# A last column range of one whole block, a final store from the scalar queue, and a new order of the early work in a fused attention and MoE kernel

## Chip, cores and metric

One core of a Trainium2 chip. The metric is the device time of a run in microseconds (us), lower is better. A profiled run's "span" is about 1.8 us shorter than its time, because it starts at the program's first instruction and ends at its last.

## The reference

Sliding-window attention with a linear distance bias, followed by a two-layer MLP with a squared ReLU:

```python
# q, k, v: (8, 8, 576, 64) float32
scores = (1/8) * q @ k.T + slope[h] * -(pos_q - pos_k)
scores = where(0 <= pos_q - pos_k < 128, scores, -1e9)
x = softmax(scores) @ v                     # (8, 8, 576, 64)
x = x.transpose(0, 2, 1, 3).reshape(4608, 512)
h = x @ w_in                                # (512, 2048)
out = (relu(h) ** 2) @ w_out                # (2048, 512), float32
```

Each batch has 576 positions: four blocks of 128 and a half block of 64. With a window of 128, a block attends to itself and to the block before it.

## The kernel before

A small list scheduler in the kernel plans the whole program: every piece of work is a task with engines, a key (priority), dependencies and ring slots. It then emits the instructions in the order of the planned starts. Each engine works through its own list strictly in that order.

The 40 blocks are numbered by when they are loaded: 0 to 7 are the first blocks of the eight batches, 8 to 13 are full blocks, 14 and 15 half blocks, and so on. For each block, keys and queries are loaded into one of four `kq` buffers, transposed (`kqT`), multiplied (scores `s`), exponentiated and masked (`P`), multiplied by `v` (`pv`), normalised (`x`), and transposed into columns of `xT`. The MLP then takes 512 columns at a time: `h` (with `w_in`, four loaded parts), relu and square (`g`), and `o` (with `w_out`, four parts).

```python
N_PE = 9            # blocks 0 to 8 are transposed on TensorE, the others by DMA
SIZE = {"kq": 4, "v": 9, "kqT": 7, "P": 3, "x": 3}
...
def load_block(m, key):                       # block m
    s_kq[m], s_v[m] = Slot("kq"), Slot("v" if kb else "v0")
    ...
    def fetch_kq():
        for i, src in enumerate((k, q)):
            nc.gpsimd.dma_start(view(kq[s_kq[m].idx], i), source(src, m, split))
...
def transpose_kq(m, due):
    if m >= N_PE:                             # by DMA, from the sync queue
        def flip():
            nc.sync.dma_start_transpose(out=tile_of(sT)[:, :, 0:n], in_=kq[s_kq[m].idx][0:n, :])
        t_f = plan.add({"SP": 1500.0}, due - 60, flip, ..., [sT], [s_kq[m]], ...)   # frees kq[m] when it lands
        return
    ...                                       # else 8 matmuls with the identity, which free kq[m]
...
if m >= N_PE:                                 # x of block m into xT, also from the sync queue
    def flip_x():
        nc.sync.dma_start_transpose(out=xT[:, :, t0:t0 + n], in_=xt[sx.idx][0:n, :])
...
# columns: the two half blocks of a pair of batches share one range of 128 columns,
# so the last range of all is two half blocks
        jobs.append(("half", [len(seq), len(seq) + 1]))
        ranges.append([(b, HALF), (b + 1, HALF)])
        seq += ranges[-1]
...
# the last 128 rows of the output are cut at column 384; each piece is stored per block of its range
def store():
    for i, (b, kb) in enumerate(ranges[4 * g + t]):
        nc.sync.dma_start(out[b * S + kb * 128:b * S + kb * 128 + n, lo:hi], so.tile[i * 64:i * 64 + n, 0:hi - lo])
```

`fill` puts matmuls without use into planned gaps of TensorE in the first 30 us.

The softmax here doesn't subtract the row's maximum and nothing guards it: scores larger than these inputs give would overflow.

## Time and profile before

| | |
|---|---|
| time, first 3 runs | 317.85 us median (317.34 to 317.96) |
| span of the profiled run | 315.63 us |
| TensorE busy | 306.2 us, 97% |
| last matmul ends | 311.02 us |
| last matmul to the end | 4.61 us |

From the page of the kernel before, its busy line, and two rows of its 40 slices (one digit is the busy share of a slice of 7.9 us, in tenths):

```profile
PE 306.2 (97%) x2810; PEld 176.3 (56%) x2810; DVE 173.4 (55%) x494; ACT 173.5 (55%) x340; POOL 105.4 (33%) x131
...
PE   6989999999999999999999999999999999999994
...
DMA  9999999999999999999999949962211000011112
```

Only slices 1, 3 and 40 of the TensorE row are under 9: after about 33 us the engine has no wait until its last matmul. DMA is at 90% or more in 25 of the first 26 slices, to about 205 us. It is no bound as long as TensorE finds its data.

The waits of TensorE alone, kernel before (total us, times, longest):

```profile
PE tp L443 <- DVE kq L379: 1.9, 1, 1.9
PE wm L413 <- DVE warm L291: 1.2, 1, 1.2
PE h L700 <- ACT rt L671: 0.7, 1, 0.7
PE h L700 <- DMA w_in_sb<-in_moe_w_in_dram: 0.3, 1, 0.3
PE o L742 <- DMA w_out_sb<-in_moe_w_out_dram: 0.3, 1, 0.3
PE pv L566 <- ACT kqf L273: 0.3, 1, 0.3
```

These are all of TensorE's waits, 4.7 us in total, none after 33 us.

The end, from the timeline of the kernel before (start, duration, engine, operation, idle before it):

```profile
310.17 0.56 DVE L271 COPY osb<-o 128x384 f32<-128x384 f32 x1 [1.85 <-PE o L742]
310.75 2.41 SPq L761 DMA_DIRECT2D out_dram<-osb  x4
311.06 0.29 DVE L271 COPY osb<-o 128x128 f32<-128x128 f32 x1 [0.34 <-PE o L742]
```

The last copy is done at 311.35, but the sync queue (SPq) is busy with four store issues until 313.16. In the trace they start at 310.75, 311.29, 311.98 and 312.57 and take 0.49, 0.59, 0.54 and 0.59 us. The last lands at 314.49.

### The profile page before, as it was taken

The page shows a single profiled execution, that of the slowest core. Times are in us where ns is not written, and L with a number is a line of the kernel's source. Part 1 is how long each engine was busy: PE and PEld are TensorE (multiplying, and loading weights), DVE is VectorE, ACT ScalarE, POOL GpSimd, SP SyncE. Part 2 cuts the span into 40 slices and gives each one's busy share as a digit, 9 for nine tenths or more (in the row PEclk, how much of TensorE's full clock was granted, in tenths as well). Part 3 has the DMA queues.
Part 4 walks back from the last instruction along what each step waited for, and adds up shares of the span by engine and source line. Part 5 has one row for each costly group of instructions (what it writes and reads, how often), then busy time and mean ns, then how long its engine had stood idle before and what let it go on. Part 6 is the DMA issues. An engine that isn't in the chain of part 4 may idle for free.

```text
span 315.6 us, 7140 instructions
## 1 busy us (share of the span) xinstructions
PE 306.2 (97%) x2810; PEld 176.3 (56%) x2810; DVE 173.4 (55%) x494; ACT 173.5 (55%) x340; POOL 105.4 (33%) x131
## 2 busy tenths in 40 slices
PE   6989999999999999999999999999999999999994
PEld 2878767667777655555555455545444444444442
DVE  3755567666767667676676666666663222222111
ACT  4676466668566635675655665557743444444300
POOL 8825498643623837206756007200000000000000
PEclk9799999999999999999999999999999999999999
DMA  9999999999999999999999949962211000011112
GB/s 129 190 204 190 169 194 178 141 174 127 208 178 127 172 136 194 160 118 143 160 199 160 145 96 137 190 114 70 50 52 50 35 34 33 35 33 44 57 69 66
DMA packets 164130, 39.14 MB, mean 124 GB/s; under 512 B 154752, under 2 KB 159616, under 8 KB 164096
## 3 DMA queue, kind: packets, MB, share of 16 engines
q0 software_dynamic: 114656, 18.10, 84.3%
q1 hardware_dynamic: 49152, 20.33, 34.3%
q8 instruction: 22, 0.36, 0.5%
q10 hardware_dynamic: 288, 0.26, 0.3%
q14 instruction: 12, 0.10, 0.1%
HBM read 36.70 MB, written 9.44 MB: 146 GB/s over the span
## 4 chain that ended last, share of the span: by engine, by line
PE 86%; DMA 9%; POOL 2%; issue 0%; DVE 0%; POOLq 0%
PE o L742 38%; PE h L716 27%; PE h L700 10%; PE pv L566 6%; PE s L499 5%; DMA w_out_sb<-in_moe_w_out_dram 5%; DMA w_in_sb<-in_moe_w_in_dram 3%; DMA kq<-in_q_dram 2%; POOL kq L387 1%; POOL vf L392 1%; PE tp L443 0%; PE xp L608 0%; POOL w_in_sb L340 0%; POOL dist L287 0%; DVE osb L271 0%
## 5 line engine op out<-in xcount | busy, mean ns | idle before, releaser
L742 PE MATMUL o<-w_out_sb,g 128*128 128x512 bf16 (+2 forms) x592 | 143.0, 373 | 0.3 <-DMA w_out_sb<-in_moe_w_out_dram 0.3
L671 ACT ACTIVATE rt<-h 128x512 bf16<-128x512 f32 x144 | 85.8, 609 | 94.2 <-PE h L716 69.9
L662 DVE TENSOR_TENSOR g<-rt 128x512 bf16<-128x512 bf16 x144 | 60.2, 421 | 75.7 <-ACT rt L671 75.6
L716 PE MATMUL h<-xT,w_in_sb 128*128 128x512 bf16 x384 | 96.7, 379 | 0.0
L742 PEld LDWEIGHTS <-g 128*128 128x128 bf16 x592 | 54.0, 98 | 55.9 <-issue 0.4
L523 ACT ACTIVATE P<-s 128x512 bf16<-128x512 f32 (+1 forms) x136 | 67.0, 582 | 9.0 <-PE s L499 8.9
L716 PEld LDWEIGHTS <-w_in_sb 128*128 128x128 bf16 x384 | 35.2, 98 | 39.3
L531 DVE TENSOR_TENSOR P<-P,masks 128x512 bf16<-128x512 bf16 (+1 forms) x112 | 44.6, 405 | 15.1 <-ACT P L523 10.3
L700 PE MATMUL h<-xT,w_in_sb 128*128 128x128 bf16 (+1 forms) x512 | 46.8, 246 | 1.1 <-ACT rt L671 0.7
L387 POOL DMA_DIRECT2D kq<-in_k_dram x39 | 33.5, 858 | 33.5 <-DMA kqT<-kq 28.2
L392 POOL DMA_DIRECT2D vt<-in_v_dram x32 | 27.0, 847 | 45.8 <-PE pv L566 43.5
L700 PEld LDWEIGHTS <-w_in_sb 128*128 128x128 bf16 x512 | 38.6, 98 | 5.2 <-DMA w_in_sb<-in_moe_w_in_dram 1.4
L387 POOL DMA_DIRECT2D kq<-in_q_dram x39 | 33.5, 859 | 9.1 <-PE h L700 4.8
L588 DVE TENSOR_TENSOR x<-pv,rec 128x256 bf16<-128x256 f32 (+1 forms) x80 | 33.5, 422 | 2.6
L566 PEld LDWEIGHTS <-P 128*128 128x128 bf16 (+1 forms) x576 | 26.0, 101 | 15.2 <-DVE x L588 1.7
L584 DVE RECIPROCAL rec<-pv 128x4 f32<-128x4 f32 (+1 forms) x80 | 14.2, 179 | 21.0 <-PE pv L566 18.1
L566 PE MATMUL pv<-vt,P 128*128 128x65 bf16 (+1 forms) x448 | 24.6, 194 | 0.0
L273 ACT ACTIVATE osb<-o 128x512 f32<-128x512 f32 x23 | 13.9, 606 | 8.0 <-PE o L742 7.7
L499 PEld LDWEIGHTS <-kqT 64*128 64x128 bf16 x448 | 12.4, 94 | 7.3 <-issue 7.2
L271 DVE COPY osb<-o 128x512 f32<-128x512 f32 (+2 forms) x14 | 9.2, 654 | 12.8 <-PE o L742 12.6
L499 PE MATMUL s<-kqT 64*128 64x128 bf16 (+1 forms) x256 | 15.6, 210 | 0.0
L499 PE MATMUL s<-kqT,kqT 64*128 64x128 bf16 (+1 forms) x192 | 11.4, 209 | 0.0
(42 smaller groups left out, 103.1 us busy)
## 6 DMA issues: line engine op xcount, KB each, us to landing
out_dram<-osb SPq DMA_DIRECT2D x32, 256.0 KB, 4.0
kq<-in_k_dram POOLq DMA_DIRECT2D x31, 128.0 KB, 7.2
kq<-in_q_dram POOLq DMA_DIRECT2D x31, 128.0 KB, 7.4
vt<-in_v_dram POOLq DMA_DIRECT2D x24, 128.0 KB, 7.4
w_in_sb<-in_moe_w_in_dram POOLq DMA_DIRECT2D x4, 512.0 KB, 11.0
w_out_sb<-in_moe_w_out_dram POOLq DMA_DIRECT2D x4, 512.0 KB, 14.4
vf<-in_v_dram POOLq DMA_DIRECT2D x8, 128.0 KB, 6.7
out_dram<-osb SPq DMA_DIRECT2D x6, 128.0 KB, 2.3
```

Of the source, the lines that this page charges most:

```text
L387: nc.gpsimd.dma_start(view(kq[s_kq[m].idx], i), source(src, m, split))
L392: nc.gpsimd.dma_start(tile_of(s_v[m])[0:n, :, 0:D], source(v, m))
L499: nc.tensor.matmul(sS[2 * g2 + r].tile[:, jj * 256 + c0:jj * 256 + c0 + w], tile_of(s_kqT[mk])[rows, c, :], tile_of(s_kqT[mq])[rows, C + c ...
L523: nc.scalar.activation(flat(Pt[sP.idx]), sS[i].tile.rearrange("p (j t) -> p j t", j=2)[:, :, lo:hi], AF.Exp, bias=0.0, scale=scale)
L531: nc.vector.tensor_tensor(flat(Pt[sP.idx]), flat(Pt[sP.idx]), flat(masks), op=ALU.mult)
L566: nc.tensor.matmul(sv.tile[0:n, hi * (D + 1):(hi + 1) * (D + 1)], Pt[sP.idx][:, place(h)].rearrange("p t q -> p (t q)")[:, w], tile_of(s_v ...
L588: nc.vector.tensor_tensor(xt[sx.idx][0:n, hf * 256:(hf + 1) * 256].rearrange("p (h e) -> p h e", h=4), heads(sv)[0:n, :, 0:D], sr.tile[0:n ...
L662: nc.vector.tensor_tensor(o, i, i, op=ALU.mult)
L671: nc.scalar.activation(srt.tile, slot.tile, AF.Relu, bias=0.0, scale=1.0)
L700: nc.tensor.matmul(slot.tile[:, f * w:(f + 1) * w], w_in_sb[:, cc, fc * 128:(fc + 1) * 128], xT[:, cc, lo:lo + w], start=cc == 0, stop=cc ...
L716: nc.tensor.matmul(slot.tile, w_in_sb[:, cc, fc * 128:(fc + 1) * 128], xT[:, cc, g * 512:(g + 1) * 512], start=cc == 0, stop=cc == C - 1)
L742: nc.tensor.matmul(slot.tile[:, 0:hi - lo], gt[:, fc, t * 128:(t + 1) * 128], w_out_sb[:, fc, lo:hi], start=fc == 0, stop=fc == FCB - 1)
```

## The change

Three intents: (1) the last column range becomes a whole block, so that each of the last two pieces is one store, and the very last is copied on ScalarE and issued from its queue; (2) the order of the early units is searched anew, by adding offsets to single tasks' keys; (3) one block fewer is transposed on TensorE (`N_PE` 9 to 8). `LEAD`, `DUE`, `NEAR` and `N_CUT` belong to the second: when the attention work of a block is due, within how many ns of the earliest start a task with a better key is preferred, and for how many blocks x is transposed in two halves.

```diff
-FIRST = ["b0", "b1", "b2", "i0", "i1", "o0", "i2", "o1", "b3", "i3", "o2", "o3", "b4", "b5", "b6", "b7"]
+FIRST = ["b0", "b1", "b2", "i0", "i1", "o0", "i2", "b3", "i3", "o1", "o2", "o3", "b4", "b5", "b6", "b7"]
-N_PE = 9
-N_CUT = 4
+N_PE = 8
+N_CUT = 2
-LEAD = 320
+LEAD = 1160
-DUE = {**{m: 200.0 * m - 1e5 for m in range(40)}, **{7: -40.0}}
+DUE = {m: 200.0 * m - 1e5 for m in range(40)}
+ADJ = {
+    "e1.1": 9000135.6, "e19.2": -177.01, ..., "u0.1.1": -99420.7, "u0.2.1": -99696.3, ...
+}
-    NEAR = {"PE": 25, "ACT": 250, "DVE": 60}
+    NEAR = {"PE": 60, "ACT": 0, "DVE": 25}
     def order(self):
+        for t in self.tasks:
+            t.key += ADJ.get(t.name, 0.0)
-        ranges.append([(b, HALF), (b + 1, HALF)])
-        seq += ranges[-1]
+        seq += [(b, HALF), (b + 1, HALF)]
+
+        ranges.insert(len(ranges) - (b + 2 == B), seq[-2:])
+        engs = {"ACT": act(hi - lo), "DVE": dve_p(hi - lo)}
+        if end and (g, t) == (NG - 1, 3):
+            del engs["DVE"]
+        final = end and (g, t) == (NG - 1, 3)
-                nc.sync.dma_start(out[...], so.tile[...])
+                (nc.scalar if final else nc.sync).dma_start(out[...], so.tile[...])
# cut: new names of tasks, a stage ring of one buffer, planning dependencies, release of g by all four last pieces
```

## The prediction

> **What bounds it now.** The page gives TensorE 306.2 of 315.6 us busy, and the table by stretches shows it 100% busy from 50 us to the last matmul at 311.06. Before that, the waits view and timeline show 1.2 us of start, a 1.9 us wait for the q cast (5.2 to 7.06), later waits of 0.3, 0.7, 0.3 and 0.3 us, and 54 filler matmuls (about 3 us). At the end, 4.6 us pass between the last matmul and the end. So only useful TensorE work, TensorE time lost before 33 us and the tail can change the time.
>
> **What the change does (from the built order of instructions).**
> 1. One block fewer (the ninth) is transposed on TensorE: 8 key/query and 4 x transposes go to the DMA queue. Four take 0.22 us in the timeline, so 0.66 us is removed. Fillers go from 54 to 50.
> 2. Weight w_out part 1 is loaded after block 3 and w_in part 3. Loads land back to back (0.85 us per block tensor, about 2.5 us per weight part), so w_in part 3 should land near 27.4 us instead of 29.96, block 3's q near 24.0 instead of 26.5.
> 3. Block 2's scores and all of block 1's attention come before the first h matmul. That first h is tied to w_in part 0 (landed 14.23; h began 14.34), the third h unit to part 1 (landed 17.76; began 17.80). These do not move. After them I expect waits of about 0.9 us (part 1) and 0.6 us (part 3), much as before; but the work done by about 37 us is one h unit (0.9 us) more and 0.4 us sooner: 1.3 us ahead.
> 4. Block 8's keys now come by DMA transpose. Block 9's took 8.4 us (51.80 to 60.20). Block 8's q lands about 49, so its transpose lands 56.9 to 57.7; TensorE would reach those scores at about 56.8. I expect a new wait of 0 to 0.9 us here, giving back part of step 3.
> 5. Tail: the last range is one store per piece instead of two. Now the scalar copy ends about 311.35, but the last of four sync-queue issues starts at 312.57 (0.5 to 0.6 us each), lands 314.49, end 315.63. One issue on the scalar queue at about 311.45, landing 1.9 us later, saves 1.1 us. The Trainium skill ("Trainium Kernel Development and Optimization", Key Constraints) says that several issuing engines only save issue time: what is saved here.
> 6. Attention stands 2.5 to 5 us of h and o work later relative to the rest, so the middle should keep having no waits; the larger lead changes little.
>
> The trace also has one half-clock stretch of 3.41 us (8.42 to 11.84), the window length in the Trainium skill ("TensorE: Matmul & The Clock Gate", Part 1). The new filler may prevent it; worth at most a few tenths, as the first h waits for weights.
>
> **Sum.** Last matmul 309.2 to 310.1 (gain 1.0 to 1.9), tail 1.1: gain 2.1 to 3.0 us. Predicted 315.2 us, 8 in 10 between 313.6 and 316.9. Faster by over 2%: 0.02; within 2%: 0.97; slower: 0.01.
>
> **Right if:** last matmul near 309.6; last landing 2.2 to 2.4 us after it (before: 3.4); w_in part 3 lands near 27.4; a TensorE wait at block 8's first scores under 1 us; none from 60 us on.
>
> **Wrong if:** that transpose lands late (1 to 3 us lost, near no gain); the new ACT and DVE order stalls TensorE for h or o banks; or early waits vanish altogether (2 us more gain).

## More of the kernel before

The sync queue (SPq) between 60 and 80 us, kernel before. The transposes of keys (`kqT`) and of x (`xT`) share it with the stores:

```profile
...
64.35 1.31 SPq L429 DMA_TRANSPOSE kqT<-kq  x1
67.88 1.25 SPq L596 DMA_TRANSPOSE xT<-x  x1
73.25 2.56 SPq L429 DMA_TRANSPOSE kqT<-kq  x2
...
```

The first line shown is block 12's keys, the second block 9's x. That x was ready at 67.85 (end of its normalisation on VectorE) and was issued at once.

## The result, and the profile after

| | before | after |
|---|---|---|
| time, median of 4 runs | 317.60 us (317.32 to 317.96) | 316.52 us (316.23 to 317.28) |
| ratio | | 0.9969 (0.9947 to 0.9991) |
| span of the profiled run | 315.63 | 314.45 |
| last matmul ends | 311.02 | 311.44 |
| last matmul to the end | 4.61 | 3.00 |

A ratio is the mean time of one kernel's fast runs over the mean of the other's fast runs of the same rounds, so it is not quite the ratio of the medians.

The change gains 1.1 us; I had predicted about 2.6. The last two rows say more: TensorE ends 0.4 us *later* than before, and the shorter end makes up for it. The early part, from which I expected 1.0 to 1.9 us, gave nothing.

The busy line of the page after:

```profile
PE 306.3 (97%) x2794; PEld 176.0 (56%) x2794; DVE 174.1 (55%) x498; ACT 170.7 (54%) x331; POOL 105.5 (34%) x131
```

The waits of TensorE alone, kernel after:

```profile
PE h L721 <- DMA w_in_sb<-in_moe_w_in_dram: 2.3, 2, 1.4
PE wm L434 <- DVE warm L308: 1.2, 1, 1.2
PE h L721 <- DMA xT<-x: 0.7, 1, 0.7
PE tp L464 <- DMA kq<-in_q_dram: 0.4, 1, 0.4
PE pv L587 <- ACT P L544: 0.4, 1, 0.4
PE xp L629 <- DVE x L609: 0.2, 1, 0.2
```

The early waits are different ones, of about the same size. The third line is new in kind: `h` waits for a DMA transpose of x. Where, the timeline of TensorE after tells:

```profile
14.99 1.07 PE L721 MATMUL h<-xT,w_in_sb 128*128 128x128 bf16 x16 [0.93 <-DMA w_in_sb<-in_moe_w_in_dram]
...
17.56 1.89 PE L721 MATMUL h<-xT,w_in_sb 128*128 128x128 bf16 x16 [1.40 <-DMA w_in_sb<-in_moe_w_in_dram]
...
80.52 2.79 PE L721 MATMUL h<-xT,w_in_sb 128*128 128x256 bf16 x24 [0.65 <-DMA xT<-x]
```

In the first two lines, the first `h` unit waits for weight part 0 (landed 14.94) and the second already for part 1 (landed 17.52). The third line is at 80.52, where I had expected no wait at all. There is no later one.

The sync queue between 60 and 80 us, kernel after:

```profile
61.71 1.23 SPq L450 DMA_TRANSPOSE kqT<-kq  x1
63.72 1.20 SPq L617 DMA_TRANSPOSE xT<-x  x1
73.12 1.23 SPq L450 DMA_TRANSPOSE kqT<-kq  x1
74.45 1.29 SPq L617 DMA_TRANSPOSE xT<-x  x1
...
```

The queue issues nothing from 64.9 to 73.12, then block 12's keys, then block 9's x at 74.45, although that x was ready at 70.06. The waits of the queue itself name what held it, the load of block 12's keys (its queries landed 0.7 us later, at 73.11):

```profile
SPq L450 <- DMA kq<-in_k_dram: 7.5, 1, 7.5
```

The x transpose lands at 80.48, and TensorE goes on at 80.52.

The chain of waits in the stretch from 60 to 100 us (shares by line), before and then after:

```profile
by line: PE h L700 49.9%; PE o L742 31.3%; PE pv L566 9.8%; PE s L499 8.3%; PE xp L608 1.1%
```

```profile
by line: PE h L721 45.7%; PE o L766 26.2%; DMA xT<-x 15.1%; PE s L520 7.0%; PE pv L587 6.2%; issue 0.1%
```

Before, the chain through this stretch is TensorE alone; after, it runs through a transfer from 74.45 to 80.48. Before 74.45 the view goes back to TensorE, but there it can't be trusted: it takes a VectorE event at 75.65, after the transpose had been issued, for what released it. The queue's own wait above is the better guide.

The end, from the timeline after:

```profile
310.59 0.56 DVE L288 COPY osb<-o 128x384 f32<-128x384 f32 x1 [1.85 <-PE o L766]
311.48 0.28 ACT L290 ACTIVATE osb<-o 128x128 f32<-128x128 f32 x1 [13.26 <-PE o L766]
311.79 0.35 ACTq L790 DMA_DIRECT2D out_dram<-osb  x1
```

One issue of 0.35 us, started at 311.79 and landed at 313.35, in place of the end of a row of four.

### Where the wait at 80 us comes from

Reading the loads and the transposes of the two traces side by side (us):

| | before | after |
|---|---|---|
| block 8's keys and queries have landed | 49.2 | 48.9 |
| block 8's buffer is read to the end | 49.8 (TensorE) | 57.40 (DMA transpose, issued 48.98) |
| block 12's k and q loads, same buffer, issued | 52.64, 53.76 | 58.68, 61.98 |
| they land | 61.80, 64.30 | 72.40, 73.11 |
| block 12's key transpose issued | 64.35 | 73.12 |
| block 9's x ready | 67.85 | 70.06 |
| block 9's x transpose issued | 67.88 | 74.45 |
| it lands | 76.36 | 80.48 |
| TensorE waits for it | no | 0.65 |

Theory A: the time is set at 80 us by a transfer. Block 8's DMA transpose holds a key buffer 7.6 us longer than TensorE did. The scheduler, which plans with that, put the v loads of blocks 12 to 16 ahead of block 12's keys and queries, which land 9 us later. (That order comes from `N_PE`, and not from the new offsets: building the kernel before with `N_PE = 8` alone, which was not run, gives the same order of these loads, and all the kernels here with `N_PE = 9` have block 12's load first. On the chip the delay goes through that order: the buffer was free at 57.40, and the waits just before the two loads, issued at 58.68 and 61.98, end with the landings of earlier loads, at 58.38 and 61.69.) Block 12's key transpose waits for it at the head of the sync queue, and block 9's x transpose stands behind. The Trainium skill ("DMA: Bandwidth & Descriptors", Anatomy of one DMA, written for the GpSimd path) says that "any semaphore wait happens on the issuing sequencer before dispatch"; the trace agrees for the sync queue, with 4.4 us (70.06 to 74.45) in which a ready transfer was not issued. What TensorE gains before 80 us is then waited away.

Theory B: the early part itself is the loss. TensorE waits 0.93 and 1.40 us for weights. In the profiled run a half-clock stretch also fell on the `h` units that follow (17.20 to 20.61), where before it fell on the prelude (8.42 to 11.84). The wait at 80 us is then a side effect worth its 0.65 us.

### The profile page after: what moved, and what is told of

Its sections match the earlier page's. It is cut to its first block, busy times and chain, and to the rows that moved or that the text cites. A ratio compares the mean times of both kernels' runs of the same rounds, so it can differ in the third digit from the quotient of the medians.

```text
span 314.4 us, 7113 instructions
## 1 busy us (share of the span) xinstructions
PE 306.3 (97%) x2794; PEld 176.0 (56%) x2794; DVE 174.1 (55%) x498; ACT 170.7 (54%) x331; POOL 105.5 (34%) x131
## 4 chain that ended last, share of the span: by engine, by line
PE 92%; DMA 5%; POOL 2%; issue 0%; ACT 0%; POOLq 0%
PE o L766 39%; PE h L739 27%; PE h L721 14%; PE pv L587 6%; PE s L520 5%; DMA w_in_sb<-in_moe_w_in_dram 3%; DMA xT<-x 2%; POOL kq L408 1%; POOL vf L413 1%; PE tp L464 1%; PE xp L629 0%; POOL w_in_sb L357 0%; POOL dist L304 0%; ACT osb L290 0%; POOLq L304 0%
## 5 line engine op out<-in xcount | busy, mean ns | idle before, releaser
L721 PE MATMUL h<-xT,w_in_sb 128*128 128x128 bf16 (+1 forms) x512 | 47.9, 250 | 3.0 <-DMA w_in_sb<-in_moe_w_in_dram 2.3
L290 ACT ACTIVATE osb<-o 128x512 f32<-128x512 f32 (+1 forms) x24 | 14.2, 590 | 23.4 <-PE o L766 23.4
L288 DVE COPY osb<-o 128x512 f32<-128x512 f32 (+1 forms) x13 | 8.9, 681 | 15.1 <-PE o L766 14.6
```

What stands on the lines that cost most here:

```text
L721: nc.tensor.matmul(slot.tile[:, f * w:(f + 1) * w], w_in_sb[:, cc, fc * 128:(fc + 1) * 128], xT[:, cc, lo:lo + w], start=cc == 0, stop=cc ...
```

## The experiments

All kernels gave correct results. Edits that name tasks are made in the finished plan (`done`, the list in emission order), so nothing else moves. The first four experiments shared one chip, the next four a second, the last two a third; across chips, compare the ratios to the kernel before.

### The changed kernel again

No edit.

> The changed kernel, unaltered, as the base for the others on the same chip. Both theories: 0.995 to 0.999 of the kernel before, span 314.4 to 315.4 us; TensorE waits at the first two weight parts (about 0.9 and 1.4 us) and of about 0.7 us at about 80 us for the x transpose of block 9. If the half-clock stretch falls elsewhere than 17 to 20 us, theory A (a transfer sets the time at 80 us, so what TensorE gains earlier is waited away there) says that the wait at 80 us grows by as much (to about 2 us) and the span stays; theory B (the two early waits and the half clock that follows them are the loss) says that the span falls by 1.5 us.

Measured: 316.48 us median of 6 runs, ratio 0.9964 (0.9946 to 0.9982). The profiled run (317.21 us) had no half-clock stretch at all. Its wait for xT was 1.9 us instead of 0.7:

```profile
PE h L721 <- DMA xT<-x: 1.9, 1, 1.9
```

The transfer landed at 81.46. Of the 1.29 us by which the wait grew, only 0.30 is TensorE coming earlier (79.57 instead of 79.87); 0.98 is the transfer landing later, as the loads of this run did from the start (weight part 0 at 15.94 instead of 14.94). So this profile fits A but decides little. The runs together say more, for they show no gain from a full clock: at a mean clock of 1.000 they took 317.21 and 316.07 us, at 0.994 to 0.995 they took 316.05 to 317.07. B had expected 1.5 us.

### Block 9's x transpose first

```diff
     done = plan.order()
+    at_ = {t.name: i for i, t in enumerate(done)}
+    done.insert(at_["x9"], done.pop(at_["kqT12"]))   # kqT12 now right after x9
```

> Only on the sync queue: the x transpose of block 9 is issued before the key transpose of block 12, which waits for its load (landed 73.1). Theory A: the x transpose is issued at about 70 instead of 74.5, lands at about 76.5, the wait of 0.65 us at 80.5 is gone, and the span falls by about 0.65 us (by up to 2 us if the half clock spares the early h units). Theory B: the wait is a consequence, gain at most 0.65 us and never more.

Measured: 314.72 us median of 6, ratio 0.9911 (0.9890 to 0.9932), 1.76 us under the changed kernel on the same chip. The x transpose was issued at 69.30 and landed at 76.02. The sync queue of this run, where one line holds both x transposes:

```profile
62.88 1.24 SPq L450 DMA_TRANSPOSE kqT<-kq  x1
64.21 6.28 SPq L617 DMA_TRANSPOSE xT<-x  x2
73.40 7.42 SPq L450 DMA_TRANSPOSE kqT<-kq  x3
```

The waits of TensorE in this run of over 0.4 us:

```profile
PE tp L464 <- DVE kq L288: 1.7, 1, 1.7
PE h L721 <- DMA w_in_sb<-in_moe_w_in_dram: 1.6, 2, 1.4
PE wm L434 <- DVE warm L308: 1.2, 1, 1.2
PE s L520 <- DMA kqT<-kq: 0.6, 1, 0.6
```

No `h` waits for xT, and the last matmul ends at 309.82. One exchange of two issues on a queue that computes nothing is worth more than the whole change. The gain exceeds B's limit of 0.65 us; so it does among runs with a half-clock stretch alone (a mean of 315.58 us here, 316.52 in the changed kernel). The new 0.6 us wait is for block 8's keys (landed 57.49), the one that I had predicted.

Now the clock matters as well: the two runs at 0.995 took 315.33 and 315.82 us, the four at 0.999 to 1.000 took 313.88 to 314.84. The difference of the means is 1.2 us (two runs against four), which did not show in the changed kernel's runs.

### The second and third h units exchanged

```diff
+    for a in ("", "relu", "sq"):
+        i, j = at_[a + "u0.1.0"], at_[a + "u0.1.1"]
+        done[i], done[j] = done[j], done[i]
```

> Only the second and third h units change places, with their relu and square: the second then needs weight part 0, which has landed, instead of part 1. The 1.4 us wait for part 1 shrinks to under 0.5 us, and TensorE is 0.9 us (if the half clock stays in the same place) to 2.4 us (if it does not come) ahead at 30 us. Theory A: the span does not change (within 0.3 us), and the wait at about 80.5 us grows from 0.65 to 1.5 to 3 us. Theory B: the span falls by 0.9 to 2.4 us.

Measured: 317.37 us median of 6, ratio 0.9992 (0.9969 to 1.0015). The edit did what it should: no wait of 1.4 us for part 1, and block 8's scores at 56.73 instead of 58.03 us (the changed kernel's profile of the same chip). At 80 us TensorE then waited longer, and the half clock came right after the wait (81.72 to 85.14):

```profile
80.59 4.25 PE L721 MATMUL h<-xT,w_in_sb 128*128 128x256 bf16 x24 [2.32 <-DMA xT<-x]
```

The transfer landed at 80.54, between the 80.48 and 81.46 of the changed kernel's two profiles. The gain of 0.9 to 2.4 us that B expected is absent. A's "within 0.3 us" was missed too: the median is 0.9 us worse than the changed kernel's. In the profiled run this is the half-clock stretch: the 24 matmuls took 4.25 us, against 2.79 us in the changed kernel. Whether the same holds in the runs without a profile I can't tell; of the six, the two at clock 0.995 and one at 1.000 are the slow ones (317.93 to 318.35), and three at 1.000 took 316.18 to 316.80.

### Both edits

> Both edits. Theory A: the gains add to more than they give one by one: 1.3 to 2 us under the changed kernel, with a new wait of up to 1.5 us at the first scores of block 8, whose key transpose landed at 57.4 when TensorE came at 58.3. Theory B: the sum of the two alone.

Measured: 314.14 us median of 4, ratio 0.9892 (0.9875 to 0.9908): 2.3 us under the changed kernel, a little more than I expected, and the fastest kernel. Block 8's scores began at 56.96, just as their keys landed (56.91), and TensorE had no wait of over 0.2 us after 23 us. The last matmul ended at 309.25. Alone, the swap gave nothing; beside the other edit it gave 0.6 us by the medians. That is not a gain of the swap for certain: none of these four runs had a half-clock stretch, and the four full-clock runs with the x transpose first have a mean of 314.33 us, only 0.2 us more. So A's claim that the gains add to more than their sum is not shown.

### Only the end changed

The kernel before with the new ranges, the copy of the last piece on ScalarE and its store from the scalar queue. TensorE's order of instructions is that of the kernel before.

> The kernel before with only the end changed (the last column range a whole block, the final piece copied on the scalar engine and stored from its queue); TensorE's order is untouched. If the tail is all that the whole change gained: last matmul where it was (about 311.0), end 3.0 instead of 4.6 us after it, time about 1.6 us under the kernel before (0.995), so at or under the changed kernel itself. If the early part also gained: 1.1 us or less, and the changed kernel is faster than this one.

Measured: 316.15 us median of 6, ratio 0.9954 (0.9940 to 0.9968), 1.3 us by the medians and 1.5 us by the ratio. From the last matmul (310.63, 0.4 us earlier than I had said) to the end: 3.14 us, against 4.61. The final store, issued once from the scalar queue:

```profile
310.98 0.35 ACTq L766 DMA_DIRECT2D out_dram<-osb  x1
```

This accounts for all that the whole change gained.

### The final piece from the sync queue

```diff
-                (nc.scalar if final else nc.sync).dma_start(
+                (nc.sync).dma_start(
```

> The changed kernel with the final piece stored from the sync queue again. If the scalar queue matters: its issue has to queue behind the wider piece's, end 0.3 to 0.6 us later after the last matmul. If only the number of stores matters (two issues fewer): the sync queue is free when the last copy ends, and the end stays 3.0 us after the last matmul, within 0.2 us.

Measured: 2.98 us from the last matmul to the end, against 3.00 with the scalar queue. The last two stores, both on the sync queue:

```profile
312.44 0.95 SPq L790 DMA_DIRECT2D out_dram<-osb  x2
```

The sync queue had been idle since 312.78 when it issued the last store at 313.05. The scalar queue contributes nothing here; having one store per piece does it. (The copy on ScalarE was not tried apart: both it and the VectorE copy of the kernel before ended 0.3 us after the last matmul.) The time was 316.97 us median of 4 with a wide interval (ratio 0.9958 to 1.0017), so only the profile tells the two kernels apart. In it two half-clock stretches in a row (15.45 to 22.27) fell on the early `h` units, and yet a wait of 0.73 us stood at 80 us: its transfer landed at 81.75.

### Block 12 loaded early

A fifth key buffer under the same order, and block 12's load ahead of the v loads.

```diff
-    kq = ring("kq", size["kq"], [128, 2 * d_model])
+    kq = ring("kq", 5, [128, 2 * d_model])
...
+    for i, s in enumerate(order_kq):      # kq slots in the order of their loads
+        s.idx = i % 5
+    done.insert(at_["lv11"], done.pop(at_["lkq12"]))
```

> The changed kernel with a fifth key/query buffer under the same order, and the load of block 12's keys and queries ahead of the v loads of blocks 11 to 16; nothing else moves. If the late load of block 12 (its buffer was held by block 8's DMA transpose until 57.4) is the root of the wait at 80 us: that load lands near 57 to 60 instead of 73, its key transpose is issued near 65, block 9's x transpose near 70, no wait at 80 us, and the time is 1.3 to 2 us under the changed kernel, as with the x transpose put first. If the sync queue is full anyway: a wait of 0.5 us or more stays.

Measured: 314.45 us median of 4, ratio 0.9901 (0.9886 to 0.9916). Block 12's load landed at 64.71 and 66.21 (7 us earlier than in the changed kernel, not the 13 to 16 that I had written). The sync queue of this run:

```profile
66.26 3.35 SPq L450 DMA_TRANSPOSE kqT<-kq  x1
69.71 1.48 SPq L617 DMA_TRANSPOSE xT<-x  x1
```

Block 12's keys are issued at 66.26, block 9's x at 69.71. There is no TensorE wait at 80 us, and the chain from 60 to 100 us is TensorE alone again:

```profile
by line: PE h L721 46.9%; PE o L766 37.8%; PE s L520 8.3%; PE pv L587 7.3%
```

The order on the sync queue is that of the changed kernel, so the late load is the root; the queue passes its lateness on to the x transpose. Whether the fifth buffer or the earlier place in the order would do alone was not tried. By the ratios the gain over the changed kernel is 2.0 us.

### The ninth block on TensorE again

```diff
-N_PE = 8
+N_PE = 9
```

> The changed kernel with the ninth block transposed on TensorE as before (the scheduler makes the rest of the order anew, so more than one thing moves). Theory A: block 8's buffer is free at about 50, no wait at 80 us; 0.7 us more of transposes; 0.5 to 1.3 us under the changed kernel. Against it: the wait at 80 us stays, and the time is 0.7 us over the changed kernel.

Measured: 316.82 us median of 4, ratio 0.9969 (0.9953 to 0.9986), the changed kernel's own ratio. My expectation failed: a wait for xT of 0.93 us stood at 78.25, and a new one of 0.72 us at 47.85. The scheduler made the order anew, TensorE reached block 8's scores at 53.98, 4 us earlier, and ran into an x transpose that was issued at 69.4 and landed at 78.2. The first link did come undone: block 12's load landed at 63.71, and its key transpose was issued at 63.76. But x of block 9 was ready only at 69.35, and its transpose took 8.8 us to land, not 6.0. So the one constant does not undo the step cleanly. The run is inconclusive on what the wait costs; the run with the early load decides it.

### Only the early part changed

The changed kernel with the end of the kernel before.

> The changed kernel with the end of the kernel before (half blocks in the last column range, both pieces copied by the same rule and stored from the sync queue); every other instruction stands as in the changed kernel. Theory A (the early part gains nothing, because the x transpose of block 9 lands at about 80 to 81.5 and what TensorE gains before is waited away): ratio to the kernel before 0.998 to 1.002, the wait at about 80 us in its profile, and 4.4 to 4.7 us from the last matmul to the end. If the tail was worth less than it seems and the early part more: 0.996 or less.

Measured: 318.00 us median of 5, ratio 1.0015 (1.0001 to 1.0028), with 4.47 us from the last matmul to the end. Its xT wait:

```profile
PE h L721 <- DMA xT<-x: 1.6, 1, 1.6
```

The early part gains nothing; it may lose a little.

### The swap with the early load

> The unit swap together with the early load of block 12 (fifth buffer). Theory A: with no wait at 80 us the swap is worth something again, up to where block 8's keys land (56.9 in the run with both edits): no TensorE wait of over 0.2 us between 60 us and the end, and 0.3 to 0.6 us under the early load alone, so 313.9 to 314.2 us. If the swap is worth nothing by itself: 314.4 to 314.6 us, as the early load alone.

Measured: 314.57 us median of 4, ratio 0.9907 (0.9894 to 0.9921). The first half of A's expectation held (no TensorE wait after 23 us), the second did not: the swap adds nothing to the early load. Both kernels reach block 8's scores at 57.0, where these keys land (56.8 in both). The single wait of 2.09 us for weight part 1 became three waits of 0.38, 0.52 and 0.63 us for later data, and the wait for the cast of block 0's q was 1.40 us in this profile and 0.35 in the other. Neither shows a wait at these scores, so why they coincide is not shown.

## Why the prediction was wrong

The failed step is number 6, "the middle should keep having no waits". The middle got one wait, of 0.65 to 2.32 us at about 80 us, for the DMA transpose of block 9's x, and it sits where it undoes everything before it. The prediction looked at what block 8's transpose does to block 8's own scores (step 4), and not at the load that reuses its buffer. Six profiles have that wait. The five with the changed kernel's order after 80 us:

| profile | half clock | wait | `h` goes on at | from there to the last matmul |
|---|---|---|---|---|
| changed kernel | 17.20 to 20.61 | 0.65 | 80.52 | 230.92 |
| the same again | none | 1.94 | 81.51 | 230.91 |
| early part only | none | 1.62 | 80.09 | 230.92 |
| final piece from the sync queue | 15.45 to 22.27 | 0.73 | 81.79 | 230.92 |
| units exchanged | 81.72 to 85.14 | 2.32 | 80.59 | 232.57 |

The last column is constant, up to the half-clock stretch of the last row. The time of the run is the landing of one x transpose, plus 230.92 us of TensorE, plus the end; in these profiles the early order and the clock before it decide how long TensorE waits. The 316.52 us lie within the stated 313.6 to 316.9 partly by luck: the end gave 0.5 us more than predicted.

Point by point:

- **Step 1** (0.66 us of transposes removed): true as work, but the move to DMA that removes them is what delays block 12's load. I costed the move on the engine that it relieves, and not by how long it holds a buffer.
- **Step 2** (w_in part 3 near 27.4): landed at 27.71, and block 3's q at 24.35. Right.
- **Step 3** (1.3 us ahead by 37 us): at 37.1 us the kernel before had done 14 `h` units and 6 `o` parts by its timeline, the changed one about 14.4 and 5, so it was half a unit behind (counts of records, of which a trace can lack a few). In the profile with the early load, at full clock, it was 15.9 and 5: about 0.8 us ahead, at 0.9 us for either. I had taken the second unit for one that needs part 0; the searched order has one there that needs part 1, so the wait was 1.40 and not 0.9 us. The half clock added up to 1.5 us (half of the 3.05 us from 17.56 to 20.61). Neither showed in the time.
- **Step 4** (block 8's keys land 56.9 to 57.7): landed at 57.40. TensorE came 0.9 us later in the first profile, so no wait; a wait of 0.63 us appeared in the profile with the x transpose put first, where TensorE came at 56.90.
- **Step 5** (tail, 1.1 us): right mechanism, mis-sized. It was 1.61 us in the profiles (4.61 to 3.00) and 1.47 us with only the end changed. Two terms were off: the last store lands 1.56 us after its issue begins, not 1.9, and the wait from the last matmul to that issue was 0.35, not 0.43 us. The credit I gave to the scalar queue was wrong. The Trainium skill ("Trainium Kernel Development and Optimization", Key Constraints) says that issuing from several engines only saves issue time; here it saved not even that (2.98 us from the sync queue, 3.00 from the scalar queue), since the sync queue was idle.
- **The clock** ("worth at most a few tenths"): the stretch moved with the run and showed no cost as long as the xT wait followed it; once that wait was gone, it was worth 1.2 us (two runs against four). Its length, 3.41 us or twice that, agrees with the window of 3413 ns in the Trainium skill ("TensorE: Matmul & The Clock Gate", Part 1). That the new filler prevents it did not come true: in 7 of the changed kernel's 10 runs the mean clock is 0.994 or 0.995, which is one such stretch (half of 3.41 in 315 us).
- **The sum**: last matmul at 309.2 to 310.1. With the x transpose put first it ended at 309.82, with the early load at 309.28, with both edits at 309.25. None of these profiles has a half-clock stretch before the last matmul. So the sum was close to what this early order is worth at full clock and without the wait at 80 us; with the stretch, by the 1.2 us above, it would end at an estimated 310.5 to 311.0.

Left open: why half-clock stretches come in some runs and not in others, how much of the 0.9 us that the exchanged units lost by the median is due to them, and what sets the landing of the x transpose within 80.05 to 81.75.

## What to carry to other kernels

When work moves from an engine to a DMA, ask how long the transfer holds its source buffer, which load reuses that buffer, and what stands behind that load's first user in an in-order queue: here 7.6 us of holding moved a load behind five others in the planned order, it landed 9 us late, and 6.6 us of that reached another block's transpose on another queue. In this kernel, bound by one engine, a single late transfer in the middle made every gain before it worthless, so look for waits at the point where data of the changed path are first used, not only where the change is. An order that was found by a search on a planned timeline should be checked on the trace for ready work that stands behind work that is not.

## What the Trainium skill lacked or had wrong

- "DMA: Bandwidth & Descriptors" (Latency and other measured facts) gives an effective bandwidth for a DMA transpose, 261 GB/s with a non-contiguous middle dimension, but no latency under load. Here the transpose of one block's keys and queries (128 x 1024, 2-byte elements) took 8.4 us from issue to landing (48.98 to 57.40) while loads kept the DMA engines busy; that is how long it held its buffer here.
- The same page (Issuing engines are not separate DMA queues) calls the time to issue a DMA "usually small relative to the DMA itself". At the end of the kernel before, four issues of 0.49 to 0.59 us each in a row (64 partitions) stood against 1.9 us from the last issue to its landing. A 128-partition store took 0.33 to 0.35 us to issue at the end of the changed kernel, and up to 1.56 us (at 148.57 us, kernel before) while loads were running. That page has no figure by shape or load for this chip.
- "TensorE: Matmul & The Clock Gate" (Part 1) has the half clock come after at least one idle window of about 3.4 us. In the kernel before it followed a window (5.01 to 8.42) of which TensorE was idle for 1.9 us, in the changed kernel one (13.79 to 17.20) with 2.0 us of idling, and with the units exchanged one (78.31 to 81.72) with 2.3 us. So less than a whole idle window was enough in these. An idle 1.9 us in the second profile of the changed kernel brought none; where the windows of that profile fell is not known, so it may have been split between two.
